# A planned fp32 kernel on one core: eight PSUM buffers of one bank in place of four of two, and the planner's tables written anew

## The chip, the cores and the metric

The kernel runs on one core of one Trainium2 chip. The metric is the device time of one launch in microseconds. Of the kernel before, three runs gave 774.08, 777.64 and 778.81 us; their median is 777.64 us.

## The reference

Everything is float32; the sequence has S = 2048 tokens, the width is D = 640, the hidden width F = 1728. A condition vector is turned into six modulation rows. The first half is a long convolution per channel (by spectra) of `shift_conv(k) * v`, gated by the modulated layer norm of q; the second half is an MLP with squared ReLU.

```python
mod = (silu(c) @ w_mod).reshape(1, 6, 1, -1)              # sa, ca, ga, sb, cb, gb
h = layernorm(q) * (1 + ca) + sa
kv = shift_conv(k, shift_k) * v                           # 4 taps along the sequence
y = irfft(rfft(pad(kv)) * rfft(pad(ssm_k)))[:, :S] + kv * ssm_D
x = q + ga * (h * y)
h = layernorm(x) * (1 + cb) + sb
out = x + gb * (relu(h @ w1 + b1) ** 2 @ w2 + b2)
```

## The kernel before

The kernel has two stages that overlap a little. The convolution stage goes over five blocks of 128 channels. For each block it loads k and v, transposes them on TensorE (`kv`, lines 758 to 799), convolves with four taps on ACT and DVE, writes the product to DRAM and reads it back in another layout (`load_x`, line 813); then come a short transform (`unit_a`, 821), the spectra (`spectra`, 843), the product of spectra (`front`, 863, on DVE and POOL), the way back (`back`, 891), transposes and a last transform (`unit_y`, 915), and the gate with q (`prep` and `finish`, 963 and 979). The MLP stage goes over eight chunks of 256 tokens. For each it normalises and transposes the tokens (`prep_hat`, `prep_xt`), and for each of 14 slices f of the hidden width it multiplies by w1 (`mlp_front`, 1090), applies bias and squared ReLU on ACT and DVE (`mlp_middle`, 1109), and accumulates the product with w2 (`mlp_back`, 1134). Each fp32 operand of the MLP is split in a high and a low part, and three products are added.

No instruction is issued where the code names it. Each call adds a node to a graph (`Graph.add`, 158): the engine, a duration from a table (`cost`, 583, or the number given to `as_one`), the buffers it reads and writes, and, for a DMA, the time of its transfer (`moved`, 570). `levels` (178) gives each node the length of the longest path behind it, to which `BIAS` (1176) adds a correction by the node's name; that is its urgency. `order` (205) then walks through time: an engine that is free takes the most urgent ready node for which buffers can be had; `lag` and `pelag` are the delays from the end of a node to the start of one that needs it, `entries` models TensorE's instruction fetch (lines 309 to 313), and each DMA starts 1.2 us after its issue or when the DMA queue is free, and is seen 0.6 us after its transfer (lines 314 to 317). At most four DMAs of the SP queue are under way. The nodes are then issued in the order of their planned start times (`emit`, 368), and every engine keeps that order (`keep_order`, 458). Semaphores are placed by the framework from the order, the tiles and the regions that are written and read.

PSUM has eight banks of 512 fp32 per partition. The planner hands them out one by one (slots B0 to B7, `one` in line 539, `banks` in line 545), and frees a bank when the last reader of what lies in it has ended. To the framework, however, they are four tiles of two banks each, `ps0` to `ps3` (line 537): banks 0 and 1 are the two halves of `ps0`, and so on. Two banks of one tile are called siblings here.

```python
bank = [ps.tile([P, 2, 512], F32, tag=f"PS{i}", name=f"ps{i}") for i in range(4)]
...
return shaped(bank[i // 2][: s[0], i % 2, : int(np.prod(s[1:]))], s)
```

In the MLP the four accumulators lie in banks 0 to 3, and the hidden slices and transposes in banks 4 to 7, taken in this order as they come free (`ACCB`, `HB`, `XTB`, line 1187).

All calls are recorded at line 375, inside `emit`, so the profile puts nearly every instruction at L375 and groups are told apart by their tiles: `ps<-xt,w_S` is a product with w1, `ps<-w_S,hring` one with w2, `ps<-a,gb` a spectrum, `ps<-cst,p` the short transform, `ps<-gi,wx` the way back, `ps<-wx,cst` and `ps<-we,cst` the last transform, `ps<-ident,...` a transpose.

Of the kernel before, what the change touches and what calls it, by code (L numbers as in the profile page):

```python
# [11 lines left out]
F32 = mybir.dt.float32  # L12
# [5 lines left out]
P = 128  # L18
# [94 lines left out]
class Graph:  # L113
# [88 lines left out]
            level[n.id] = top + n.cost + n.dma  # L202
            n.prio = level[n.id] + self.bias.get(n.key[0], 0.0) + self.bias.get(n.key, 0.0)

    def order(self, lag=0.1, pelag=0.2, patience=0.0, trace=None):
        self.levels()
        nodes, bufs = self.nodes, self.bufs
        owner = {}
# [64 lines left out]
        dma_free, landed = 0.0, []  # L273
# [6 lines left out]
        while done < len(nodes):  # L280
            moved = False
            for e in ready:
                while free[e] <= t + 1e-9:
                    if e == "SP" and len(landed) >= OUT and landed[-OUT] > t:
                        break
                    pick = None
                    for k, (pr, i) in enumerate(ready[e]):
                        if nodes[i].lock and port[0] > t + 1e-9 and port[1] != e:
                            continue
                        got = place(nodes[i])  # L290
                        if got is not None:
                            pick = k
                            break
                    if pick is None:
                        break
                    if patience and e == "PE":
                        wait = [w for w, pr2, j in soon[e] if t < w < t + patience and pr2 < pr]
                        if wait:
                            heapq.heappush(events, (min(wait), -1))
                            break  # L300
                    n = nodes[ready[e].pop(pick)[1]]
                    for b, ci in got:
                        taken[b.n] = ci
                        for s in b.choices[ci][0]:
                            owner[s] = b.n
                    end = t + n.cost
                    if n.lock:
                        port = (end, e)
                    if e == "PE":
                        ent += n.entries  # L310
                        if ent >= 256:
                            end = max(end, block + 4.0)
                            block, ent = end, ent - 256
                    if n.dma:
                        start = max(t + 1.2, dma_free)
                        dma_free = start + n.dma
                        land = dma_free + 0.6
                        heapq.heappush(events, (land, -1))
                        if e == "SP":
                            landed.append(land)  # L320
                        free[e] = t + n.cost
                        end = land
                    else:
                        free[e] = end
                    heapq.heappush(events, (free[e], -1))
                    out.append((t, end, n))
                    done += 1
                    moved = True
                    for i in n.next:
                        l = 0.0 if nodes[i].engine == e and not n.dma else pelag if e == "PE" else lag  # L330
                        when[i] = max(when[i], end + l)
                        need[i] -= 1
                        if not need[i]:
                            heapq.heappush(events, (when[i], i))
                            if patience:
                                soon[nodes[i].engine].append((when[i], -nodes[i].prio, i))
                    for b in n.bufs:
                        b.left -= 1
                        b.end = max(b.end, end + (pelag if e == "PE" else lag))
                        if not b.left:  # L340
                            heapq.heappush(events, (b.end, -2 - b.n))
            if done == len(nodes):
                break
            if not events:
                stuck = [(nodes[i].calls[0][1], [b.name for b in nodes[i].bufs if taken[b.n] is None])
                         for r in ready.values() for _, i in r][:20]
                self.need, self.ready = need, ready
                raise RuntimeError(f"no way on: {stuck}")
            t = max(t, events[0][0])
            while events and events[0][0] <= t + 1e-9:  # L350
                _, i = heapq.heappop(events)
                if i >= 0:
                    n = nodes[i]
                    bisect.insort(ready[n.engine], (-n.prio, i))
                    if patience:
                        soon[n.engine] = [x for x in soon[n.engine] if x[2] != i]
                elif i < -1:
                    b = bufs[-2 - i]
                    for s in b.choices[taken[b.n]][0]:
                        if owner.get(s) == b.n:  # L360
                            owner[s] = None
            if len(landed) >= OUT and landed[-OUT] > t:
                heapq.heappush(events, (landed[-OUT], -1))
# [70 lines left out]
def ssm_mlp_kernel(  # L434
# [99 lines left out]
    KN = [part(lambda: KV, 1024 + 1024 * i, (f"KN{i}a", f"KN{i}b")) for i in range(4)]  # L534
    UT = [part(lambda: KV, 3072 + 512 * i, (f"KN{2 + i // 2}{'ab'[i % 2]}",)) for i in range(4)]
    KVALL = (("KA0", "KA1") + tuple(f"KN{i}{h}" for i in range(4) for h in "ab"), lambda s, d, n: sb.tile(s, d, tag="KV", name=n))
    bank = [ps.tile([P, 2, 512], F32, tag=f"PS{i}", name=f"ps{i}") for i in range(4)]

    def one(i):
        def make(s, d, n):  # L540
            return shaped(bank[i // 2][: s[0], i % 2, : int(np.prod(s[1:]))], s)

        return ((f"B{i}",), make)

# [28 lines left out]
        return n / run * (0.0095 + 4.1e-5 * run) / 16  # L573

    def sp_dma(o, i, run):
        g.add("SP", 0.06, (sp_issue, "dma", (o, i), {}), [x for x in (o,) if isinstance(x, View)],
              [x for x in (i,) if isinstance(x, View)], dma=moved(o, i, run))

    def act_dma(o, i, run):
# [3 lines left out]
    def cost(engine, op, args, kw):  # L583
        o = args[0]
        n = o.ix.size if op != "bn_stats" else args[1].ix.size
        ins = [a for a in args[1:] if isinstance(a, View)]
        deep = any(a.buf.psum for a in ins)
        if engine == "ACT":
            given = any(isinstance(kw.get(x), View) for x in ("scale", "bias"))
            return (0.38 if given else 0.19) + 0.00083 * n  # L590
        if engine == "DVE":
            if op == "bn_stats":
                return 0.15 + 0.001 * n
            if op in ("tensor_mul", "tensor_add", "tensor_sub") and not deep:
                return 0.1 + 0.00115 * n
            if op == "bn_aggr":
                return 0.21
            return 0.19 + 0.0011 * n
        if n < 200 or op == "tensor_copy":
            return 0.36  # L600
        return 0.1 + 0.0023 * n
# [20 lines left out]
        g.add("PE", 0.0, (nc.tensor.matmul, "matmul", (o, a, b), dict(start=start, stop=stop)), [o], ins, entries=n, hold=hold)  # L622

    def turn(o, x, hold=()):
        g.add("PE", 0.0, (nc.tensor.transpose, "transpose", (o, x, ident), {}), [o], [x], entries=4, hold=hold)

    def copy(eng, o, i, hold=()):
        if eng is act:
# [72 lines left out]
    def mod_col(j, dst, plus):  # L701
        a = mod_sum(j)
        g.key = ("mr", j)
        t = psum(f"mc_{j}", (P, NB), ONE)
        with g.as_one(1.8):
            for b in range(NB):
                mm(t[:, b : b + 1], a[:, b * P : (b + 1) * P], ones[:, 0:1], True, True)
        dve.tensor_scalar(dst, t, float(plus), None, op0=ALU.add)
# [112 lines left out]
    def unit_a(b, i, n):  # L821
        g.key = ("pa", b)
        t = [psum(f"pa_{b}_{i}_{n}_{e}", (P, 8, 32, 2), PAB) for e in range(2)]
        for half in range(2):
            with g.as_one(0.51):
                for j in range(4 * half, 4 * half + 4):
                    for e in range(2):
                        l = slice(64 * e, 64 * e + 64)
# [86 lines left out]
    def unit_y(b, l):  # L915
# [14 lines left out]
        u = U[b, l]  # L930
        raw = b < 2
        d = sbuf(f"y_{b}_{l}", (P, 4, P), [quarter(f"UP{i}", n) for i in range(2) for n in range(4)]) if raw else u
        with g.as_one(0.87):
            if not raw:
                g.use(g.group, u, False)
            for h in range(2):
# [135 lines left out]
    def prep_xt(n, b):  # L1072
# [3 lines left out]
        t = psum(f"xtp_{n}_{b}", (P, 2, P), XTB if n else ANY, "xtp")  # L1076
        f = sbuf("xf", (P, CH), ML["xf"])
        for i in range(2):
            with g.as_one(0.13):
                turn(t[:, i], ML["xh"][i][:, b * P : (b + 1) * P])  # L1080
        t2 = t.rearrange("p i s -> p (i s)")
        c1, c0 = cbs[:, 1, b : b + 1], cbs[:, 0, b : b + 1]
# [70 lines left out]
    def mlp_out(n):  # L1153
# [20 lines left out]
                sp_dma(osrc[a, :, 2 * n : 2 * n + 2], X1t[n][32 * a : 32 * a + 32], 5120)  # L1174

    BIAS = {
# [3 lines left out]
        ("mr", 3): 145, ("ms", 1): -5, "pa": 90, "pac": 160, ("pra", 4): 5, ("prm", 0): 35, ("prm", 4): -100,  # L1180
        "prp": 30, ("prp", 1): -90, ("prp", 2): -5, ("prp", 4): -85, "qp": 120, "qpc": 220, "st1": 260,
        "st1e": -20, "st2": -105, ("t", 1): 100, ("t", 3): 105, ("t", 4): 40, "tc": 65, "vt": -20,
        ("vt", 2): -60, "wh": 230, "wl": -285, "x": 110, "y": -50,
    }

    KVB, PAB, XB, QB = ANY[::-1], ANY, ANY, ANY[2:6][::-1]
# [76 lines left out]
    for i in range(2):  # L1263
        o = slice(320 * i, 320 * i + 320)
        t = psum(f"gr_{i}", (P, 320), ONE)
        for b in range(NB):
            with g.as_one(0.56):
                mm(t, gv[:, b], gw[:, b, o], b == 0, b == NB - 1)
        copy(act, row0b[:, o], t)
    mul(pool, row1b, row1b, row0b)  # L1270
# [85 lines left out]
```

## Time and profile before

| what | value |
|---|---|
| median of three runs | 777.64 us |
| the profiled execution, its own time | 776.13 us |
| its span, first to last instruction | 774.3 us |
| PE (matmul) busy | 667.8 us, 86% |
| DVE, ACT, POOL busy | 391.0, 326.8, 253.7 us |
| mean granted clock of TensorE | 0.970 |
| moved by DMA | 74.46 MB |

The profile's page has the busy time of each engine, the span in 40 slices, the DMA queues, the chain of work that ended last and the costliest groups. A group's line reads: line, engine, operation, what it writes and reads, shape, count, then busy microseconds, mean nanoseconds of one, and the idle time of the engine just before them with what ended it. The table of windows gives the busy time of each engine in a stretch, the granted clock and the share of time that the DMA engines were busy. The view of waits names who waited for whom, in total, how often, and the longest. The timeline lists instructions in order, with idle time and releaser in brackets.

### The profile page before, as it was taken

How to read it: one execution, taken by the hardware profiler on the slowest of the kernel's cores; microseconds unless marked ns; L12 is line 12 of the kernel's file. 1: busy time of each engine (PE TensorE's matmuls, PEld its weight loads, DVE VectorE, ACT ScalarE, POOL GpSimd, SP SyncE). 2: the span in 40 equal slices, each digit the busy share in tenths (PEclk: the TensorE clock that was granted, in tenths of full speed). 3: DMA queues.
4: the chain of work that ended last, by engine and by line, in shares of the span. 5: the costliest groups of instructions: out<-in, count | busy, mean ns of one | idle time of the engine just before them, and what ended most of it. 6: DMA issues, size and time to landing. Idle time of an engine off the chain costs nothing. (4 is left out here: it accounts for less than half of the span.)

```text
span 774.3 us, 17837 instructions
## 1 busy us (share of the span) xinstructions
PE 667.8 (86%) x7509; PEld 583.5 (75%) x7509; DVE 391.0 (50%) x780; ACT 326.8 (42%) x678; POOL 253.7 (33%) x316
## 2 busy tenths in 40 slices
PE   3777878768776788889999899999999999898996
PEld 2676766756665576659898778898898988788896
DVE  4526267467844457667425525626455356254451
ACT  3343755547766666556422412423323224133220
POOL 1106566036669555843500400402204004003001
PEclk9689999989999989999999999999999999999999
DMA  9699699599481752646002002002020020010011
GB/s 236 192 238 269 150 252 238 156 199 240 101 174 36 176 110 83 195 133 176 1 1 69 2 1 69 0 1 69 1 69 1 1 69 1 1 46 23 1 35 35
DMA packets 109124, 74.46 MB, mean 96 GB/s; under 512 B 49266, under 2 KB 96370, under 8 KB 108788
## 3 DMA queue, kind: packets, MB, share of 16 engines
q1 hardware_dynamic: 107088, 72.87, 36.6%
q8 instruction: 59, 0.97, 0.6%
q10 hardware_dynamic: 1892, 0.44, 0.3%
q14 instruction: 21, 0.17, 0.1%
q0 software_dynamic: 64, 0.01, 0.0%
HBM read 58.88 MB, written 14.42 MB: 95 GB/s over the span
## 5 line engine op out<-in xcount | busy, mean ns | idle before, releaser
L375 PE MATMUL ps<-xt,w_S 128*128 128x512 f32 (+1 forms) x935 | 174.0, 332 | 14.7 <-ACT mtmp L375 6.6
L375 PEld LDWEIGHTS ps<-xt,w_S 128*128 128x128 f32 x935 | 139.4, 188 | 39.2 <-ACT mtmp L375 12.1
L375 PE MATMUL ps<-w_S,hring 128*128 128x320 f32 x648 | 108.6, 312 | 0.2
L375 PE MATMUL ps<-a,gb 128*64 128x128 f32 x1280 | 83.0, 284 | 21.2 <-DVE wx L375 10.5
L375 PEld LDWEIGHTS ps<-w_S,hring 128*128 128x128 f32 x648 | 98.2, 188 | 2.1 <-DVE mtmp L375 0.7
L375 PEld LDWEIGHTS ps<-a,gb 128*64 128x64 f32 x1280 | 72.9, 142 | 33.2 <-DVE wx L375 12.1
L375 ACT ACTIVATE mtmp<-ps,b1t 128x256 f32<-128x256 f32 (+1 forms) x112 | 51.6, 472 | 93.4 <-PE ps L375 55.3
L375 DVE TENSOR_TENSOR mtmp<-ps,mtmp 128x256 f32<-128x256 f32 (+1 forms) x99 | 41.0, 420 | 73.9 <-PE ps L375 41.9
L375 ACT ACTIVATE hring<-mtmp 128x256 fp32r<-128x256 f32 x74 | 30.7, 415 | 108.8 <-PE ps L375 101.5
L375 POOL TENSOR_TENSOR wx<-wx 128x256 f32<-128x256 f32 x80 | 60.3, 774 | 41.6 <-DVE wx L375 40.8
L375 POOL TENSOR_TENSOR x<-mtmp,x 128x640 f32<-128x640 f32 (+1 forms) x9 | 13.3, 1486 | 183.3 <-DVE mtmp L375 183.3
L375 PE MATMUL ps<-cst,p 64*64 64x64 f32 x2560 | 54.9, 236 | 17.2 <-issue 5.0
L375 DVE TENSOR_TENSOR wx<-ps,wx 128x512 f32<-128x512 f32 x64 | 42.0, 686 | 50.6 <-PE ps L375 33.1
L375 PEld LDWEIGHTS ps<-cst,p 64*64 64x64 f32 x2560 | 48.0, 148 | 25.1 <-issue 9.1
L375 DVE TENSOR_TENSOR hring<-mtmp,hring 128x256 fp32r<-128x256 f32 x74 | 36.3, 495 | 58.9 <-ACT hring L375 58.6
L375 ACT ACTIVATE a<-ps 128x512 f32<-128x512 f32 x80 | 45.9, 631 | 40.0 <-PE ps L375 39.2
L375 POOL TENSOR_TENSOR x<-x,gb2row 128x640 f32<-128x640 f32 x16 | 25.6, 1611 | 98.5 <-ACT mtmp L375 70.5
L375 PE MATMUL ps<-w_S,w_W 128*128 128x320 f32 x312 | 51.4, 311 | 0.4 <-DVE mtmp L375 0.2
L375 PE MATMUL ps<-gi,wx 64*128 64x128 f32 x640 | 45.0, 292 | 4.8 <-ACT q L375 1.8
L375 PEld LDWEIGHTS ps<-gi,wx 64*128 64x128 f32 x640 | 41.3, 202 | 9.1 <-ACT q L375 4.1
L375 PEld LDWEIGHTS ps<-w_S,w_W 128*128 128x128 f32 x312 | 46.8, 188 | 1.4 <-DVE mtmp L375 1.2
L375 DVE SCALAR_TENSOR_TENSOR mtmp<-mtmp 128x256 f32<-128x256 f32 x91 | 46.6, 517 | 2.1
(128 smaller groups left out, 1004.7 us busy)
## 6 DMA issues: line engine op xcount, KB each, us to landing
wm<-in_w_mod_dram SPq DMA_DIRECT2D x25, 320.0 KB, 4.4
KV<-in_A_k_dram SPq DMA_DIRECT2D x20, 256.0 KB, 4.2
KV<-in_A_v_dram SPq DMA_DIRECT2D x20, 256.0 KB, 4.2
p<-in_A_ssm_k_dram SPq DMA_DIRECT2D x20, 256.0 KB, 4.6
p<-kv_d SPq DMA_DIRECT2D x20, 256.0 KB, 4.4
xp<-in_A_q_dram SPq DMA_DIRECT2D x20, 256.0 KB, 5.9
out_dram<-x SPq DMA_DIRECT2D x28, 160.0 KB, 2.6
w1s<-in_B_w_dram SPq DMA_DIRECT2D x13, 320.0 KB, 3.1
```

Of the source, the lines that this page charges most:

```text
L375: fn(*real, **{k: a.real() if isinstance(a, View) else a for k, a in kw.items()})
```

## The change

Each bank becomes a tile of its own, and the numbers that the planner works with are replaced: the delays between nodes, the start and landing of a DMA, the time that SP needs to issue one, the durations of ACT and DVE instructions and of some groups of matmuls, the fetch entries of a transpose, and the whole table of corrections. No arithmetic, no loop and no buffer in SBUF is changed.

```diff
-    def order(self, lag=0.1, pelag=0.2, patience=0.0, trace=None):
+    def order(self, lag=0.06, pelag=0.1, patience=0.0, trace=None):
...
-                        start = max(t + 1.2, dma_free)
+                        start = max(t + 1.4, dma_free)
...
-                        land = dma_free + 0.6
+                        land = dma_free + 0.7
...
-    bank = [ps.tile([P, 2, 512], F32, tag=f"PS{i}", name=f"ps{i}") for i in range(4)]
+    bank = [ps.tile([P, 512], F32, tag=f"PS{i}", name=f"ps{i}") for i in range(8)]
...
-            return shaped(bank[i // 2][: s[0], i % 2, : int(np.prod(s[1:]))], s)
+            return shaped(bank[i][: s[0], : int(np.prod(s[1:]))], s)
...
-        g.add("SP", 0.06, (sp_issue, "dma", (o, i), {}), [x for x in (o,) if isinstance(x, View)],
+        g.add("SP", 0.4, (sp_issue, "dma", (o, i), {}), [x for x in (o,) if isinstance(x, View)],
...
-            given = any(isinstance(kw.get(x), View) for x in ("scale", "bias"))
-            return (0.38 if given else 0.19) + 0.00083 * n
+            given = sum(x in kw and not isinstance(kw[x], float) for x in ("scale", "bias"))
+            return (0.18, 0.26, 0.39)[given] + 0.00083 * n
...
-            return 0.19 + 0.0011 * n
+            return 0.17 + 0.001 * n if op != "scalar_tensor_tensor" else 0.17 + 0.00112 * n
...
-        g.add("PE", 0.0, (nc.tensor.transpose, "transpose", (o, x, ident), {}), [o], [x], entries=4, hold=hold)
+        g.add("PE", 0.0, (nc.tensor.transpose, "transpose", (o, x, ident), {}), [o], [x], entries=2, hold=hold)
...
-        with g.as_one(1.8):
+        with g.as_one(1.2):
...
-            with g.as_one(0.51):
+            with g.as_one(0.49):
...
-        with g.as_one(0.87):
+        with g.as_one(0.91):
...
-            with g.as_one(0.13):
+            with g.as_one(0.11):
...
     BIAS = {
-        "b1": -210, "comb": 25, ("f1", 0): 100, ("f1", 4): -5, "f2": -5, ("f2", 6): 5, ("fin", 3): 15,
...
+        "b1": 40, ("comb", 3): 40, "f2": -170, "fin": -160, ("fin", 0): -10, "gate": -185, "h": 40,
+        ("h", 1): 215, "hat": 155, ("kn", 4): -25, ("ks", 0): 10, "kst": 335, ("kt", 3): 95, ("kt", 4): 60,
...
-            with g.as_one(0.56):
+            with g.as_one(0.53):
```

The last pair is the group of the gate row's matmuls; the rest of the two correction tables, 47 entries before and 44 after, is left out.

More of the change, by code (lines that the diff above doesn't have):

```diff
@@ L1176, in ssm_mlp_kernel @@
     BIAS = {
[3 rows of a table removed]
[L1180 to L1183, printed above, removed]
+        "b1": 40, ("comb", 3): 40, "f2": -170, "fin": -160, ("fin", 0): -10, "gate": -185, "h": 40,
+        ("h", 1): 215, "hat": 155, ("kn", 4): -25, ("ks", 0): 10, "kst": 335, ("kt", 3): 95, ("kt", 4): 60,
+        ("lh", 3): -10, ("lh", 4): -15, ("lm", 1): 20, ("lm", 3): 40, ("mr", 1): -40, ("mr", 2): 15,
+        ("mr", 4): 160, "mul": 40, ("mul", 2): 100, ("pa", 1): 60, "pac": -5, ("pac", 1): -55, ("pac", 2): 5,
+        ("pac", 3): 190, ("prm", 0): 40, "prp": -130, "qp": 490, ("qpc", 0): -5, ("st1", 10): 205, "tc": 225,
+        ("vt", 2): -105, "wl": -240, ("wl", 6): -130, ("wl", 7): -85, ("x", 0): -10, "xt": 610, "y": -40,
+        ("y", 0): -85, ("yc", 1): 90, ("yc", 4): 55,
     }
```

2 rows, old and new, of the table BIAS are left out of this document.

## The prediction

> **What bounds the kernel now.** I read the page first (which engine is nearest to full), then the table of windows (where that engine idles), then TensorE's waits (what ends its idle time), then the timeline at single waits.
>
> ```profile
> span 774.3 us, 17837 instructions
> ...
> PE 667.8 (86%) x7509; PEld 583.5 (75%) x7509; DVE 391.0 (50%) x780; ACT 326.8 (42%) x678; POOL 253.7 (33%) x316
> ```
>
> ```profile
> 0.00:20.00 20.00, 6.27 (x37) 5.69 (x38) 9.03 (x22) 6.38 (x12) 3.04 (x12) 0.94 1.05 238
> 20.00:200.00 180.00, 144.01 (x2976) 119.68 (x2976) 97.53 (x183) 94.64 (x179) 76.65 (x132) 0.91 0.84 212
> 200.00:350.00 150.00, 118.67 (x1998) 95.10 (x1999) 88.35 (x139) 96.36 (x195) 95.97 (x94) 0.97 0.49 125
> 350.00:768.20 418.20, 398.84 (x2501) 363.07 (x2499) 194.37 (x438) 129.44 (x294) 77.16 (x78) 1.00 0.10 29
> 768.20:774.30 6.10, 0.00 (x0) 0.00 (x0) 1.68 (x4) 0.00 (x0) 0.85 (x2) 0.82 0.38 108
> ```
>
> The columns of a window are its length, the busy time of PE, weight loads, DVE, ACT and POOL, the clock, the DMA share and GB/s. PE is the busiest engine in every window but the first and the last, and idles for 774.3 - 667.8 = 106.5 us: 13.7 in the head, 36.0 and 31.3 in the two parts of the convolution, 19.4 in the MLP, 6.1 in the tail. Up to 200 us the DMA engines are busy for 0.84 of the time, so there a second limit stands close. What ends PE's idle time:
>
> ```profile
> PE ps L375 <- ACT wx L375: 16.3, 14, 3.9
> PE ps L375 <- DVE wx L375: 14.9, 17, 3.1
> PE ps L375 <- ACT mtmp L375: 7.7, 19, 0.6
> PE ps L375 <- DMA KV<-in_A_k_dram: 7.5, 1, 7.5
> PE ps L375 <- DVE mtmp L375: 7.3, 15, 0.7
> PE ps L375 <- issue: 6.8, 6, 2.2
> PE ps L375 <- ACT a L375: 6.3, 8, 1.2
> PE ps L375 <- DVE kacc L375: 6.0, 3, 4.6
> PE ps L375 <- ACT we L375: 5.7, 5, 1.7
> PE ps L375 <- ACT q L375: 3.6, 6, 1.2
> PE ps L375 <- DVE KV L375: 3.3, 3, 1.6
> PE ps L375 <- DVE xfs L375: 3.0, 6, 0.7
> ```
>
> The nine rows with ACT or DVE, kacc left out, sum to 68.1 us. They name instructions that read PSUM. One such wait, in the MLP:
>
> ```profile
> 453.37 0.85 PE L375 MATMUL ps<-xt,w_S 128*128 128x512 f32 x4
> 454.25 0.47 ACT L375 ACTIVATE mtmp<-ps,b1t 128x256 f32<-128x256 f32 x1 [1.29 <-PE ps L375]
> 454.78 0.65 PEld L375 LDWEIGHTS ps<-xt,w_S 128*128 128x128 f32 x4 [0.88 <-ACT mtmp L375]
> 454.78 0.96 PE L375 MATMUL ps<-xt,w_S 128*128 128x256 f32 x4 [0.56 <-ACT mtmp L375]
> 455.85 0.42 DVE L375 TENSOR_TENSOR mtmp<-ps,mtmp 128x256 f32<-128x256 f32 x1 [2.37 <-PE ps L375]
> 456.33 0.62 PE L375 MATMUL ps<-xt,w_S 128*128 128x256 f32 x2 [0.59 <-DVE mtmp L375]
> ```
>
> PE does four matmuls of one slice and stops until ACT has read another slice; it does four more and stops until DVE has read it. The five pairs of a slice go to one bank that nobody reads yet, so no data asks for this stop in the middle. It is the tile of two banks: the reader was queued behind PE's work on its sibling, and PE's next matmul behind the reader.
>
> **The change part by part.**
>
> *Eight tiles of one bank.* I followed the semaphores through both built programs, from each wait to the instruction that ends it. Before, PE has 346 waits for a reader of PSUM; in 185 (105 in the convolution, 80 in the MLP) that reader is later than the last reader of PE's own bank. In the changed program it is 16 of 394. On the other side, 235 of 329 waits of ACT and DVE on PE name a later matmul than the last one into the bank that is read; in the changed program 12 of 371. So the change does do what it says. The price of the false waits is in the trace: I matched each idle stretch of PE over 40 ns to the instruction that ended it. The 185 account for 102 stretches and 69.1 us: 22.8 before 200 us, 28.4 from there to 350, 17.9 in the MLP. That agrees with the nine rows' 68.1.
>
> Not all comes back, since behind a false wait may stand a true one. I wrote the old order into eight tiles, took the waits that then remain at the stalled matmul and the eleven behind it, and gave each the end of its instruction in the trace. Directly free are 11.2, 10.7 and 12.9 us, 34.8 in sum. That is a lower figure for the same order, because those readers were themselves late by the 235 waits. An example of one that stays:
>
> ```profile
> 269.60 0.49 ACT L375 ACTIVATE KV<-xp,nm,rs 128x128 f32<-128x128 f32 x1 [5.17 <-DMA xp<-in_A_q_dram]
> 270.00 0.57 ACT L375 ACTIVATE wx<-ps 128x512 f32<-128x512 f32 x1
> 270.63 1.12 PE L375 MATMUL ps<-we,cst 128*64 128x512 f32 x1 [3.73 <-ACT wx L375]
> ```
>
> ACT stood 5.17 us behind a load in its own queue; PE then needed wx as data. Only another order helps here.
>
> MLP: between 12.9 and 17.9 us of idle, plus what a stop costs inside busy time (0.96 against 0.85 us for the same four matmuls above, 0.11 times 46 stretches = 5.1), so 13 to 23. I take 18, near the whole idle time, since DVE and ACT are busy for 46% and 31% of that window and keep up. Convolution: between 11 (half of what is directly free, if the loads bind) and 51.2 us (all). I take 29: 11 before 200 us, where the DMA share of 0.84 leaves 0.16 x 180 = 29 us at the very most, and 18 of the 28.4 after it, where DMA is at 0.49 and no engine above 80%.
>
> *More waits.* PE's waits on ACT and DVE rise from 409 to 455, since one wait on a pair used to cover two banks. Where a wait is already met it is hidden under the matmul before it; uncovered it costs the step that the chain of work shows after a release, 0.04 us:
>
> ```profile
> 663.54 0.48 ACT mtmp L375
> 664.03 0.04 issue
> 664.07 0.98 PE ps L375 x4
> ```
>
> 46 x 0.04 = 2 us as a bound; I take 0.
>
> *The table of durations.* It adds no instruction: both programs have 5203 matmuls, 675 ACT, 780 DVE and 314 POOL instructions and the same 283 DMAs. It works through the order alone. Against the trace:
>
> ```profile
> L375 ACT ACTIVATE mtmp<-ps,b1t 128x256 f32<-128x256 f32 x104 | 47.9, 472 | 86.8 <-PE ps L375 50.3 <-DVE hring L375 19.7 <-DVE w_W L375 6.4
> L375 DVE TENSOR_TENSOR wx<-ps,wx 128x512 f32<-128x512 f32 x64 | 42.0, 686 | 50.6 <-PE ps L375 33.1 <-ACT wx L375 13.0 <-POOL wx L375 2.0
> L375 DVE TENSOR_SCALAR xfs<-ps,cbs 128x256 f32<-128x256 f32 x38 | 19.9, 538 | 18.4 <-PE ps L375 9.6 <-ACT mtmp L375 4.7 <-POOL xt L375 2.7
> 18.12 0.34 SPq L564 DMA_DIRECT2D gb<-in_gb_dram  x1
> ```
>
> The bias activation goes from 592 to 472 ns (measured 472), the product of spectra from 753 to 682 (686), an SP issue from 60 to 400 (340); one moves away, the tensor_scalar from 472 to 426 (538). On balance the plan comes nearer to the chip. Worth 0 in the sum; in the range -8 (waits like the one at 270 us planned away: those at 166 and 270 cost 3.9 and 3.7) to +8 (two new ones of that size).
>
> *Corrections and order.* They move nodes on all five engines, DMAs on SP's queue included. Program order of the first loads (eight of k and v, then the spectra's input) and of the end (134 products with w2 after the last product with w1) is nearly the same, so head (13.7) and tail (6.1) are left as they are; bounds -3 and +3 from the row of the first load, 7.5 us. In the MLP the new order takes w1's products in runs of 20 where the old often had 10. POOL's queue has the same instructions and is busy for 43% to 64% of the convolution windows, so I price its moves at nothing; if that cover goes, a late combination of spectra costs its own length per block.
>
> *The clock.* The largest stalls are followed by a lower clock:
>
> ```profile
> 260.00:270.00 10.00, 5.19 (x84) 3.71 (x76) 2.47 (x5) 4.43 (x10) 6.86 (x6) 1.00 1.10 230
> 270.00:280.00 10.00, 8.99 (x92) 7.20 (x94) 4.14 (x6) 5.50 (x13) 3.54 (x3) 0.66 0.29 82
> ```
>
> 0.66 over 10 us costs 3.4 us at most. I count 1 us for the convolution as a whole (0 to 6). The Trainium skill, "TensorE: Matmul & The Clock Gate", section "HAM oscillation", says that idle gaps beyond about 3.4 us throttle the engine again; by that rule the stalls of 3.9 and 3.7 us are the ones that count, the trace agrees, and as these wait for data the gain would be nearer 0.
>
> Sum: 18 + 29 + 1 = 48 us from the profiled execution's 776.1 gives 728. That execution is 1.5 us under the median of the three runs (777.64), against which it is 6.4% less.
>
> **The rivals.**
>
> *The convolution keeps its time.* The loads bind before 200 us and data waits after it. For: the DMA share of 0.84, and only 21.9 of 51.2 us directly free. Against: 16% slack and the late readers. MLP 18 and some 4 of the convolution: 754.
>
> *The order is better throughout.* 23 + 51 + 6 = 80: 696. Against: it leaves PE hardly more idle than head and tail (667.8 + 13.7 + 6.1 = 688).
>
> *Slower: the loads come late.* For each block, PE's short transform needs eight loads in p, and SP has at most four under way. With an order that asks for them one place later each is late by its time to land:
>
> ```profile
> p<-in_A_ssm_k_dram SPq DMA_DIRECT2D x20, 256.0 KB, 4.6
> p<-kv_d SPq DMA_DIRECT2D x20, 256.0 KB, 4.4
> ```
>
> All 40 late by 4.5 us with nothing to cover would be 180 us; 48 us, or 11 of them, undo the gain. 16 of 40: 728 + 72 = 800. Against it: PE waits for such a load once now, and the new plan expects 2.1 us of overhead instead of 1.8.
>
> *The clock falls with eight buffers in turn.* If the MLP's clock of 1.00 fell to the 0.93 that stands in the row below, 418 x 0.07 = 29 us come on top: 757.
>
> ```profile
> 170.00:180.00 10.00, 9.09 (x112) 7.53 (x112) 5.48 (x10) 6.51 (x14) 5.39 (x14) 0.93 0.93 216
> ```
>
> Against it: the clock is 1.00 in the MLP with its 46 short stalls, and these become fewer. The same page of the Trainium skill, section "A second HAM failure mode: psum-queue depth-cycling", tells of a kernel that cycles through PSUM banks with micro-idles and oscillates; by that rule this change is a danger, but the trace shows micro-idles at full clock.
>
> *No change.* The waits that fall were covered by others: 776, though 34.8 us are directly free.
>
> **How the numbers follow.** Forecast 0.65, the convolution keeps its time 0.14, better throughout 0.08, late loads 0.05, the clock 0.04, no change 0.04. The first two, the third and the clock are faster by over 1% (about what a measurement of this kernel can tell from no change): 0.91; same 0.04; slower 0.05. The forecast's own range is from 13 + 19 = 32 to 23 + 41 = 64 us: 712 to 744. With the rival at 754 and 8 us for the order at the lower end, the range is 704 to 756, and leaves out about 0.2.
>
> **What would show it.** The split: PE's waits on ACT mtmp and DVE mtmp nearly gone, and PE's idle time in the MLP under 5 us. The convolution: PE idle between 20 us and the first products with w1 at some 38 us instead of 67, with the DMA share before 200 us rising above 0.84. The order: no load among PE's largest waits after the head. Wrong would be an unchanged number of short stops in the MLP, or a convolution whose idle time is ended by data or loads to the same total.

## The result, and the profile after

The changed kernel takes 712.21 us (median of four runs, 710.54 to 714.11) against 776.34 us of the kernel before on the same chip; the ratio is 0.9174, with a 95% interval of 0.9134 to 0.9214. The profiled execution took 712.65 us, 63.5 us less than the one profiled before (776.13). Ratios and intervals here and below count fast executions alone; slow is one that lies more than 1.5% above the fastest of its kernel, as two of the four of experiment e4 do.

The head of the profile's page after, and its table of windows (length, then busy time of PE, weight loads, DVE, ACT and POOL, then clock, DMA share and GB/s):

```profile
span 710.9 us, 17833 instructions
...
PE 650.5 (92%) x7509; PEld 581.9 (82%) x7509; DVE 381.3 (54%) x780; ACT 328.6 (46%) x678; POOL 253.1 (36%) x316
```

```profile
0.00:20.00 20.00, 9.33 (x72) 8.42 (x76) 10.01 (x25) 7.03 (x14) 3.81 (x15) 0.91 1.00 216
20.00:200.00 180.00, 153.78 (x3438) 129.94 (x3431) 103.13 (x191) 112.81 (x214) 93.58 (x144) 0.93 0.86 222
200.00:306.00 106.00, 91.31 (x1444) 71.68 (x1445) 73.06 (x116) 73.48 (x147) 73.70 (x77) 0.95 0.59 157
306.00:705.00 399.00, 396.09 (x2569) 371.86 (x2567) 193.69 (x448) 135.24 (x305) 81.37 (x82) 1.00 0.12 32
705.00:710.90 5.90, 0.01 (x1) 0.00 (x0) 1.45 (x4) 0.00 (x0) 0.63 (x1) 0.87 0.40 111
```

The first product with w1 starts at 306.0 us; before it started at 338.7. I take it as the border of the two stages, and for the comparison the same two windows of the kernel before:

```profile
0.00:338.70 338.70, 259.30 (x4940) 211.85 (x4941) 187.31 (x329) 190.13 (x371) 169.98 (x234) 0.93 0.71 178
338.70:768.20 429.50, 408.49 (x2571) 371.70 (x2569) 201.98 (x449) 136.68 (x309) 82.84 (x83) 1.00 0.11 32
```

The convolution is 32.7 us shorter (PE idle 79.4 before, 51.6 after), the MLP 30.5 us (PE idle 21.0 before, 2.9 after). In the MLP only 18.1 us of this were idle time; PE's busy time fell by 12.4 us as well, though the matmuls are the same. TensorE's waits after:

```profile
PE ps L375 <- issue: 12.3, 11, 2.9
PE ps L375 <- DMA KV<-in_A_k_dram: 8.2, 3, 7.5
PE ps L375 <- DMA p<-kv_d: 6.4, 3, 3.0
PE ps L375 <- ACT q L375: 6.2, 5, 1.9
PE ps L375 <- DVE KV L375: 5.6, 2, 3.1
...
PE ps L375 <- ACT a L375: 2.3, 4, 1.1
...
PE ps L375 <- ACT wx L375: 1.2, 4, 0.4
PE ps L375 <- ACT mtmp L375: 1.1, 2, 0.9
...
PE ps L375 <- DVE mtmp L375: 0.8, 3, 0.4
...
PE ps L375 <- DVE wx L375: 0.5, 1, 0.5
```

The two longest rows of before, ACT wx and DVE wx (16.3 and 14.9 us), are at 1.2 and 0.5, and the 34 short stops for mtmp (15.0 us) at 5 (1.9 us). What is left is the first load, stops for which the profile shows no releaser ("issue"), loads, and data. The "issue" stops went from 6.8 to 12.3 us, most of them before products of the short transform; what they are was not settled.

### The profile page after: what moved, and what is told of

It is laid out like the page before. It is cut to its first block, busy times and chain, and to the rows that moved or that the text cites. A ratio compares the mean times of both kernels' runs of the same rounds, so it can differ in the third digit from the quotient of the medians.

```text
span 710.9 us, 17833 instructions
## 1 busy us (share of the span) xinstructions
PE 650.5 (92%) x7509; PEld 581.9 (82%) x7509; DVE 381.3 (54%) x780; ACT 328.6 (46%) x678; POOL 253.1 (36%) x316
## 4 chain that ended last, share of the span: by engine, by line
PE 69%; DMA 20%; DVE 5%; issue 2%; ACT 1%; SPq 1%; POOL 0%; DVEq 0%; ACTq 0%; POOLq 0%
PE ps L375 69%; DMA wm<-in_w_mod_dram 4%; DMA q<-in_A_q_dram 2%; DMA KV<-in_A_k_dram 2%; DMA kv_d<-KV 2%; DMA gb<-in_gb_dram 2%; DMA p<-kv_d 2%; DMA w2s<-in_B_w_dram 1%; DVE mtmp L375 1%; SPq L564 1%; DMA xp<-in_A_q_dram 1%; DVE KV L375 1%; DMA p<-in_A_ssm_k_dram 1%; DMA KV<-in_A_v_dram 1%; DVE s L375 1%
## 5 line engine op out<-in xcount | busy, mean ns | idle before, releaser
L375 PE MATMUL ps<-xt,w_S 128*128 128x512 f32 (+1 forms) x935 | 161.2, 328 | 0.9 <-ACT mtmp L375 0.9
L375 PE MATMUL ps<-w_S,hring 128*128 128x320 f32 x648 | 106.3, 311 | 0.0
L375 ACT ACTIVATE mtmp<-ps,b1t 128x256 f32<-128x256 f32 (+1 forms) x112 | 51.8, 472 | 49.8 <-DVE hring L375 21.6
L375 PE MATMUL ps<-cst,p 64*64 64x64 f32 x2560 | 51.4, 236 | 16.2 <-issue 8.3
L375 DVE TENSOR_TENSOR hring<-mtmp,hring 128x256 fp32r<-128x256 f32 x74 | 34.1, 469 | 55.4 <-ACT hring L375 55.2
L375 ACT ACTIVATE w_W<-mtmp 128x256 fp32r<-128x256 f32 (+1 forms) x38 | 15.8, 417 | 71.5 <-PE ps L375 71.3
L375 PE MATMUL ps<-gi,wx 64*128 64x128 f32 x640 | 41.0, 278 | 3.5 <-ACT q L375 3.3
L375 DVE SCALAR_TENSOR_TENSOR mtmp<-mtmp 128x256 f32<-128x256 f32 x91 | 42.8, 471 | 2.4
```

The source lines that it names most:

```text
L375: fn(*real, **{k: a.real() if isinstance(a, View) else a for k, a in kw.items()})
```

## The experiments

In a diff below, "-" is the kernel named at its head. Stage times are of the profiled execution, borders as above.

**e1: the old order in eight tiles.** From the kernel before:

```diff
-    bank = [ps.tile([P, 2, 512], F32, tag=f"PS{i}", name=f"ps{i}") for i in range(4)]
+    bank = [ps.tile([P, 512], F32, tag=f"PS{i}", name=f"ps{i}") for i in range(8)]
...
-            return shaped(bank[i // 2][: s[0], i % 2, : int(np.prod(s[1:]))], s)
+            return shaped(bank[i][: s[0], : int(np.prod(s[1:]))], s)
```

> The kernel before with one edit: eight tiles of one bank; the planner's numbers, corrections and so the order stay as before. Theory 1 (the waits on the sibling bank cost the time, the new plan little): PE's short stops in the MLP go, its MLP stage falls from 429 to about 400 us and the convolution from 339 to 310 to 320, together 720 to 732. Theory 2 (the new plan brought most of the gain): only what is directly free of the idle time comes back, 35 us, so about 741.

Measured: 711.13 us, ratio 0.9134 (0.9089 to 0.9180), convolution 305.6, MLP 400.2. The two lines alone give all that the whole change gives. Theory 1 holds and was still too careful: the total lies under its 720 to 732, the convolution under its 310 to 320.

```profile
0.00:305.60 305.60, 255.79 (x4940) 212.25 (x4941) 192.35 (x330) 191.12 (x371) 172.75 (x234) 0.93 0.78 197
305.60:705.80 400.20, 396.34 (x2571) 371.49 (x2569) 204.27 (x448) 136.17 (x308) 85.00 (x83) 1.00 0.12 34
```

**e2: the new order in four tiles.** The same two lines put back in the changed kernel.

> The changed kernel with one edit: the four tiles of two banks are put back under the new plan. Theory 1: the stops on the sibling come back in both stages; 755 to 772. Theory 2: most of the gain stays; 725 to 745. If the two parts need each other, this is at or above the 776 of before while the old order in eight tiles gains little.

Measured: 785.21 us, ratio 1.0111 (1.0053 to 1.0168); convolution 346.8, MLP 431.5. All of the gain is gone, and the new plan with paired banks is about 1% slower than the old one, beyond what theory 1 expected.

```profile
0.00:346.80 346.80, 262.85 (x4942) 211.51 (x4943) 186.63 (x329) 192.58 (x373) 170.07 (x234) 0.94 0.71 175
346.80:778.30 431.50, 410.51 (x2569) 371.54 (x2567) 193.02 (x448) 135.43 (x307) 81.42 (x81) 1.00 0.11 30
```

With e1 this makes a square: 777 and 785 in four tiles, 711 and 712 in eight. That the two parts need each other is refuted by e1, which gains everything without the new plan.

**e4 and e10: half of the banks apart.** From the kernel before, with banks 4 to 7 as four tiles of their own (e4), or banks 0 to 3 (e10); e4's edit:

```diff
-    bank = [ps.tile([P, 2, 512], F32, tag=f"PS{i}", name=f"ps{i}") for i in range(4)]
+    bank = [ps.tile([P, 2, 512], F32, tag=f"PS{i}", name=f"ps{i}") for i in range(2)]
+    lone = [ps.tile([P, 1, 512], F32, tag=f"PS{i}", name=f"ps{i}") for i in range(4, 8)]
...
-            return shaped(bank[i // 2][: s[0], i % 2, : int(np.prod(s[1:]))], s)
+            t, j = (bank[i // 2], i % 2) if i < 4 else (lone[i - 4], 0)
+            return shaped(t[: s[0], j, : int(np.prod(s[1:]))], s)
```

> The kernel before with banks 4 to 7 as tiles of their own, banks 0 to 3 still two tiles of two; plan as before. The MLP's hidden slices and transposes lie in banks 4 to 7, its accumulators in 0 to 3. If the stops in the MLP come from the hidden slices' siblings alone, the MLP stage falls by the same 28 to 30 us as with all eight apart, and the convolution, which uses all banks, by about half as much as there: 735 to 745. If the accumulators' pairs matter too, the MLP stage falls by less than 20: above 748.

> The kernel before with banks 0 to 3 as tiles of their own and banks 4 to 7 left as two tiles of two: the reverse of e4. The MLP's hidden slices are read in 4 to 7, so its stage should stay at 425 to 430; the convolution gets the rest of what it gained with all eight (e4 left it at 330 of 306 to 339), 318 to 332 if the two halves add up. Total 750 to 768.

Measured: e4 736.58 us as the median of all four runs, ratio 0.9405 (0.9336 to 0.9474) from the two shorter ones (728.02 and 734.10 us), MLP 401.2, convolution 330.0; e10 751.01 us, ratio 0.9653 (0.9590 to 0.9715), MLP 426.8, convolution 317.9. The profiled run of e4 is one of the two longer ones (739.06 us). If the shorter ones differ from it in the convolution, theirs takes 319 to 325 us; this is an estimate from the run times. In the MLP the hidden slices' banks are all of it: 28 of 29 us with 4 to 7 apart, 3 with 0 to 3 apart. In the convolution both halves bring something: e10 gains 20.8 of e1's 33.1 us, e4 8.7 in its profiled run and by the estimate 14 to 20 in its shorter ones. Which half brings more is not shown.

**e5, e6 and e9: one kind of wait at a time.** From e1: while the nodes are issued, each PSUM access notes its bank, and a dependency on the sibling is added. In e5 it goes from a matmul to the last ACT and DVE readers of the sibling, in e6 from a reader to the last matmul into the sibling, in e9 both.

```diff
                 fn(*real, **{k: a.real() if isinstance(a, View) else a for k, a in kw.items()})
+                self.sibling(n, args)
+
+    def sibling(self, n, args):
+        ins = self.nc.cur_bb.bb.instructions[-1]
+        at = lambda v: int(v.buf.choices[self.place[v.buf.n]][0][0][1:])
+        if n.engine == "PE":
+            b = at(args[0])
+            for name in self.reads.get(b ^ 1, {}).values():
+                self.tie(ins, name)
+            self.wrote[b] = ins.name
+            return
+        for v in args[1:]:
+            if isinstance(v, View) and v.buf.psum:
+                b = at(v)
+                if (b ^ 1) in self.wrote:
+                    self.tie(ins, self.wrote[b ^ 1])
+                self.reads.setdefault(b, {})[n.engine] = ins.name
```

(`tie` adds a synchronising dependency; e5 is without the two lines that use `wrote`, e6 without the two that loop over `reads`.) Counted in the built programs, TensorE's waits on the sibling are 185 in e5 and e9, as before, and 14 in e6; the readers' late waits are 239 in e6 and e9 (235 before) and 16 in e5.

> The old order in eight tiles (711.1 us in its own run), with a dependency added from each matmul to the last ACT and DVE readers of the sibling bank: TensorE's 185 waits on the sibling are back, the readers wait for their own bank alone. Theory 1 (TensorE's stops are the whole cost): nearly all of the 66 us return, 755 to 778. Theory 2 (the two kinds of wait feed each other: a reader held up by the sibling's matmuls is what makes TensorE's wait for it long): a reader that starts as soon as its own bank is done is often through by the time TensorE asks, so less than half returns, 715 to 742.

> The old order in eight tiles, with a dependency added from each ACT or DVE reader of PSUM to the last matmul into the sibling bank: the readers' late waits are back (239 against 235 before), TensorE's waits are on its own bank alone. Theory 1: ACT and DVE have room (under 60% busy), so 711 to 722. Theory 2: readers up to a group of matmuls late delay what needs their results, in the convolution above all: 722 to 745, and what this and the run beside it return adds up to clearly less than 66 us, the rest being their feeding each other.

> The old order in eight tiles with both kinds of dependency on the sibling bank added (those of e5 and of e6). Theory 2 (the two kinds feed each other; nothing else of the two-bank tile counts): the whole 66 us return although each alone returned 9 and 16, so 770 to 785 and an MLP stage near 429. Rival (the tile itself costs something else, such as its addresses, or the framework's wait placement): between 736, the plain sum, and 765.

Measured: e5 720.09 us, ratio 0.9258 (0.9204 to 0.9311), MLP 403.5; e6 726.84 us, ratio 0.9351 (0.9298 to 0.9403), MLP 404.2; e9 769.30 us, ratio 0.9890 (0.9818 to 0.9962), MLP 427.5. TensorE's waits alone return 9 us, the readers' alone 16, both together 58. Theory 2 holds for e5 and e6; e9 lies just under its 770 and above the rival's 765, and its MLP stage (427.5 for an expected 429) decides for theory 2:

```profile
0.00:333.80 333.80, 261.42 (x4940) 215.06 (x4941) 186.24 (x330) 190.57 (x371) 170.68 (x234) 0.92 0.72 180
333.80:761.30 427.50, 408.28 (x2571) 371.77 (x2569) 201.81 (x447) 136.23 (x308) 81.83 (x82) 1.00 0.11 32
```

One passage of the MLP, with the same instructions in the same order, shows why. In e9 it is as in the kernel before (timeline shown in the prediction):

```profile
447.46 0.85 PE L375 MATMUL ps<-xt,w_S 128*128 128x512 f32 x4
448.34 0.47 ACT L375 ACTIVATE mtmp<-ps,b1t 128x256 f32<-128x256 f32 x1 [1.29 <-PE ps L375]
448.87 0.96 PE L375 MATMUL ps<-xt,w_S 128*128 128x256 f32 x4 [0.57 <-ACT mtmp L375]
449.94 0.42 DVE L375 TENSOR_TENSOR mtmp<-ps,mtmp 128x256 f32<-128x256 f32 x1 [2.37 <-PE ps L375]
450.42 0.61 PE L375 MATMUL ps<-xt,w_S 128*128 128x256 f32 x2 [0.58 <-DVE mtmp L375]
450.87 0.59 PE L375 MATMUL ps<-w_S,hring 128*128 128x320 f32 x3
```

In e6 the readers still stand behind the matmuls (1.30 and 1.55 us), but TensorE goes on:

```profile
422.06 1.92 PE L375 MATMUL ps<-xt,w_S 128*128 128x512 f32 x10
422.96 0.48 ACT L375 ACTIVATE mtmp<-ps,b1t 128x256 f32<-128x256 f32 x1 [1.30 <-PE ps L375]
423.73 0.42 DVE L375 TENSOR_TENSOR mtmp<-ps,mtmp 128x256 f32<-128x256 f32 x1 [1.55 <-PE ps L375]
423.82 0.60 PE L375 MATMUL ps<-w_S,hring 128*128 128x320 f32 x3
```

In e5 ACT does not wait for the matmuls, so it has read its bank by the time that TensorE asks for it:

```profile
415.86 2.00 PE L375 MATMUL ps<-xt,w_S 128*128 128x512 f32 x10
416.01 0.48 ACT L375 ACTIVATE mtmp<-ps,b1t 128x256 f32<-128x256 f32 x1 [0.55 <-DVE hring L375]
416.52 0.42 DVE L375 TENSOR_TENSOR mtmp<-ps,mtmp 128x256 f32<-128x256 f32 x1 [0.55 <-ACT mtmp L375]
417.70 0.60 PE L375 MATMUL ps<-w_S,hring 128*128 128x320 f32 x3
```

And in e1 neither waits for the other:

```profile
411.11 1.92 PE L375 MATMUL ps<-xt,w_S 128*128 128x512 f32 x10
411.25 0.47 ACT L375 ACTIVATE mtmp<-ps,b1t 128x256 f32<-128x256 f32 x1 [0.55 <-DVE hring L375]
411.76 0.42 DVE L375 TENSOR_TENSOR mtmp<-ps,mtmp 128x256 f32<-128x256 f32 x1 [0.54 <-ACT mtmp L375]
412.86 0.60 PE L375 MATMUL ps<-w_S,hring 128*128 128x320 f32 x3
```

From the first matmul of the passage to the first product with w2 behind it: 3.41 us in e9 (450.87 - 447.46), 1.76 in e6, 1.84 in e5, 1.75 in e1. In this passage each kind of wait alone runs in the shadow of other work; together they are a handshake, in which reader and matmuls take turns.

e9 ends 8 us below the 777 of before, 5 us of it in the convolution (333.8 against 338.7). The copy of the waits is not exact (TensorE's waits on its own bank are 184 in e9 and 161 before); what the rest is was not settled.

**e3, e11 and e12: the planner's numbers.** All have eight tiles and the old corrections; e3 has all new numbers, e11 the new delays alone (`lag`, `pelag`, DMA start and landing, SP issue), e12 the new durations and fetch entries alone.

```diff
-    def order(self, lag=0.1, pelag=0.2, patience=0.0, trace=None):
+    def order(self, lag=0.06, pelag=0.1, patience=0.0, trace=None):
...
-                        start = max(t + 1.2, dma_free)
+                        start = max(t + 1.4, dma_free)
...
-                        land = dma_free + 0.6
+                        land = dma_free + 0.7
...
-        g.add("SP", 0.06, (sp_issue, "dma", (o, i), {}), [x for x in (o,) if isinstance(x, View)],
+        g.add("SP", 0.4, (sp_issue, "dma", (o, i), {}), [x for x in (o,) if isinstance(x, View)],
```

This is e11 against e1; e12 has the other lines of the change instead, e3 both.

> The changed kernel with the old table of corrections of urgency; eight tiles and the new durations stay. Theory 1: the order matters little, so 712 to 732, and the MLP stage stays near 400. Rival (the corrections carry the convolution's gain): the convolution stage is back at 325 or more, the total above 735.

> Old corrections, old durations and eight tiles, with the new delays between nodes, DMA start and landing and SP issue time alone. With all new numbers the old corrections gave 722, with all old ones 711. If any new set of numbers spoils corrections that were fitted to the old ones: 716 to 730. If the delays are nearer to the chip and that counts: 700 to 710, a version better than both.

> Old corrections, old delays and eight tiles, with the new durations of ACT, DVE, transposes and matmul groups alone. If any new set of numbers spoils the fit: 716 to 730. If the durations are what helps: 700 to 710.

Measured: e3 722.03 us (ratio 0.9293, 0.9258 to 0.9327), e11 740.07 (0.9526, 0.9477 to 0.9574), e12 734.00 (0.9455, 0.9403 to 0.9508). The MLP stage is 400.4, 397.1 and 399.8, the convolution 313.7, 336.5 and 324.5 against 305.6 in e1. The new numbers make this plan worse by 11 to 29 us as long as the old corrections stay, e11 and e12 by more than the bounds of their expectations; with the new corrections the loss is gone, and the changed kernel is where e1 is. Of the numbers compared with the trace in the prediction, most are nearer to it than the old ones; the delays of e11 were not compared, the SP issue apart. e3 kept within theory 1's total, but its premise, that the order matters little, fell: in these three runs it moves the convolution by up to 31 us and the MLP by 3 at most.

```profile
0.00:336.50 336.50, 259.26 (x4948) 216.05 (x4948) 200.16 (x345) 200.85 (x389) 177.78 (x237) 0.90 0.75 190
```

In this row of e11 no engine works more than in e1's by over 10 us; PE idles 77.2 us against 49.8, at a granted clock of 0.90 against 0.93.

**e7 and e8: six loads under way.** e1 (e7) and the changed kernel (e8) with a new plan for it:

```diff
-OUT = 4
+OUT = 6
```

> The old numbers and corrections in eight tiles with OUT = 6 in place of 4: up to six DMAs of the SP queue under way, the plan made anew for it. If the loads now bind the convolution (its DMA share was 0.84 already before): its 306 us fall by 8 to 20, total 692 to 704. Rival (the engines of DMA are what is full, not the places in the queue; or the order suffers): 706 to 725.

> The changed kernel with OUT = 6 in place of 4, the plan made anew with the new numbers and corrections. If the loads bind: 692 to 705. Rival: 707 to 725. If this and the run beside it go different ways, it is the order that decides and not the number of loads under way.

Measured: e7 735.21 us (ratio 0.9450, 0.9403 to 0.9497), e8 721.70 (0.9263, 0.9210 to 0.9315); convolution 327.3 and 308.1. Six loads under way with these corrections do not help: e7 is slower than even the rival had it, and e8 lies in the rival's bounds. As the plan changed with the number of places, and a changed order alone cost up to 29 us in e11, the two runs do not show whether the places would hold the convolution in an unchanged order; that stays open. No version was found that beats both kernels: e1 and the changed kernel are the same within their intervals.

## Why the prediction was right, and where its terms were off

The sum was 48 us, and 63.5 were measured in the profiled execution; 712.2 us lies in the range (704 to 756) and at the lower edge of the forecast's own (712 to 744). The mechanism was right. Most of the 15 us that the sum missed are one term, the MLP's.

*Eight tiles.* Right, and shown: e1 isolates it, e2 takes it away, e5, e6 and e9 rebuild it. The direct figure of 34.8 us was rightly called a lower one, for the reason given there: readers late by their own false waits. How much that is I did not size; 9 + 16 = 25 us come from the two kinds by themselves, and 58 - 25 = 33 us from their feeding each other; the last 8 of the 66 us are open, as said under e9.

*MLP, 18 us (13 to 23).* Mis-sized: 30.5 measured, 29.3 in e1. The idle part was right (18.1 us). The step that failed is the price of a stop inside busy time, taken as 0.11 us from two rows of four matmuls. In the passage above TensorE loses 3.41 - 1.75 = 1.66 us, and the rows show 0.57 + 0.58 = 1.15 us as idle: 0.51 us for two stops, 0.26 each. Over the whole stage I compared the starts of neighbouring matmuls with the median of the same pair of shapes. The pairs across the 53 stops of over 40 ns in the kernel before, with the pair right behind each, lose 34.7 us, of which 20.9 are shown as idle: again 0.26 us a stop. The changed kernel has 8 such stops, which lose 4.4 us; the difference, 30.3 us, is the stage's whole gain.

The 0.26 us have two parts. The pairs across the stops lose 29.5 us, so 0.16 us a stop come ahead of it, and 0.10 behind it: in the passage of e9 the first matmul after a stop is followed 0.227 us later by the next one, in e1 the same one 0.118 us later. The prediction's 0.11 is this second part alone. What it left out is the first, which can be read in the groups' rows of before (the last figure ahead of the second bar is the mean length of one in ns):

```profile
L375 PE MATMUL ps<-xt,w_S 128*128 128x512 f32 x385 | 139.1, 397 | 2.3 <-DVE mtmp L375 1.7 <-ACT mtmp L375 0.4
L375 PE MATMUL ps<-xt,w_S 128*128 128x256 f32 x550 | 122.2, 287 | 12.4 <-ACT mtmp L375 6.2 <-DVE mtmp L375 2.9 <-DVE xfs L375 2.1
```

A pair of the two shapes is shown 397 + 287 = 684 ns long, but five pairs took 1.75 us in e1, 350 ns each. In the rows, matmuls overlap by about half: behind one of 128x512, shown 397 ns long, the next starts after 233 ns (median). Idle time is counted from the end of the last one shown, so the overlap that a stop destroys, 397 - 233 = 164 ns here, stays inside "busy".

*Convolution, 29 us (11 to 51), and clock, 1 us.* Measured 32.7 together, 33.1 in e1, so the size was nearly right; the make-up was not, and that the sum came so close is in part luck. The forecast took its 29 us from idle time and left the head as it was. Of the 32.7 us, 27.8 are idle time, 3.0 of them in the head, and 4.9 are PE's busy time. The split was to be 11 before and 18 after 200 us. As e1 keeps the old order, it can be read there: the matmul that starts at 199.3 us in the kernel before starts at 182.7 in e1, 16.6 us earlier (2.0 of them by 20 us), and the first product with w1 33.1 us earlier. So it is 16.6 before and 16.5 after, and the loads held the first part back less than assumed; the DMA share up to 200 us rose from 0.84 to 0.86. PE idles 40.9 us between 20 us and the first product with w1; some 38 were foretold.

The clock's mean over the convolution went from 0.93 to 0.94, and stayed at 0.93 in e1. The reading that the stalls of 3.9 and 3.7 us are the ones that count for it does not hold: in the changed kernel no stop of PE behind the head is longer than 3.1 us, and its clock still falls to half six times between 50 us and the MLP, for 3.4 to 6.8 us each. Two of these, at stops of 2.4 and 2.9 us:

```profile
54.10:57.30 3.20, 3.04 (x24) 2.70 (x25) 0.01 (x1) 1.99 (x5) 1.62 (x6) 0.50 0.83 219
225.00:231.00 6.00, 2.96 (x109) 2.80 (x108) 1.71 (x1) 4.20 (x9) 3.46 (x3) 0.50 0.90 203
```

*More waits, 0 us.* Nothing in the runs speaks against it; it was not tried alone.

*The table of durations and the corrections, 0 us (-8 to +8).* The sum is right (711.1 without them, 712.2 with them) and the reason was wrong. I argued that a plan nearer to the chip does little either way. e3, e11 and e12 show harm of 11, 29 and 23 us by numbers without their corrections, beyond my 8; the new corrections only pay that back.

*The rivals.* "The convolution keeps its time" is refuted by 32.7 us. "Better throughout" (696) asked for all of the convolution's false waits; 51.6 us of idle time stay there. "Late loads" is there on a small scale: waits for p<-kv_d went from 0.5 to 6.4 us (1.5 in e1), so the sign that no load stands among PE's largest waits after the head did not come. The clock stayed at 1.00 in the MLP with eight buffers in turn, so the danger that the Trainium skill names in "TensorE: Matmul & The Clock Gate", section "A second HAM failure mode: psum-queue depth-cycling", did not come about here.

By the Trainium skill ("PSUM — Partial Sum Buffer", section "PSUM bank collisions raise a hardware error"), accesses of two engines to different banks run clean side by side; by this a wait on the sibling bank protects nothing. The traces agree so far as such accesses overlap in e1 without any loss of pace, 1.75 us for the ten matmuls with ACT and DVE reading the sibling meanwhile.

## What to carry to other kernels

A buffer's unit of synchronisation should be no larger than the unit in which it is handed out: a tile of two banks ties two producers and two readers that have nothing to do with each other, and it cost some 66 of 777 us here. When many short stops of the busiest engine are ended by readers, follow the semaphore of one to its instruction and ask whether data or only the tile joins the two; then judge both directions together, since each alone may be hidden. Corrections tuned on a planner's numbers belong to those numbers: change one set alone and the plan may be worse than with both wrong.

## What the runs showed of the hardware that was not expected

A stop of TensorE costs 0.26 us more than the idle time that the profile shows for it, in this stage of matmuls with 256 to 512 columns, at full clock: 0.16 are overlap lost ahead of the stop, 0.10 a slower start behind it. The granted clock fell to half six times in the changed kernel's convolution behind the head although no stop there was longer than 3.1 us, and stayed at 1.00 in the MLP of the kernel before with 53 stops of 0.39 us in the mean. ACT and DVE reading one bank while TensorE writes its neighbour did not slow either: the ten matmuls of the passage start at the same distances, to 2 ns, in e1, where ACT reads from 0.14 us on, and in e6, where it reads from 0.90 us on; the bias activation took 0.47 to 0.48 us and the addition 0.42 us with and without matmuls running, in e1, e5 and e9 alike.
